# Dividing one expansion of queries by bank pairs around a turn of x, in a polysketch attention + GELU MLP kernel

## The chip, the cores and the metric

The kernel runs on one core of one Trainium2 chip. A core has several engines that run at the same time, each with its own queue of instructions: TensorE (PE in the profile, with its weight loads as PEld), VectorE (DVE), ScalarE (ACT), GpSimd (POOL), and SyncE (SP), which here only issues DMAs. TensorE writes its products to PSUM, a memory of eight banks per partition, and VectorE or ScalarE reads them from there. The metric is the device time of one execution, in microseconds (us); lower is better.

## The reference, cut to what matters

```python
# attention: q, k, v of (batch 4, heads 4, tokens 1088, 32), sketches S1, S2 of (8, 32)
def phi(x):
    a = einsum('rd,bhsd->bhsr', S1, x)
    b = einsum('rd,bhsd->bhsr', S2, x)
    return einsum('bhsi,bhsj->bhsij', a, b).reshape(..., 64)
q_p, k_p = phi(q), phi(k)
kv  = einsum('bhsf,bhsd->bhfd', k_p, v);  z = sum(k_p, axis=2)
num = einsum('bhsf,bhfd->bhsd', q_p, kv)
den = einsum('bhsf,bhf->bhs', q_p, z)[..., None] + 1e-06
x   = (num / den) -> (batch*tokens, heads*32) = (4352, 128)
# MLP: w_in (128, 2048), w_out (2048, 128)
h   = x @ w_in
out = (0.5 * h * (1 + erf(h / sqrt(2)))) @ w_out
```

Every token gets 64 features, the products of two sketches of length 8. Attention is linear: keys and values are first summed to a 64 x 32 table per head (`kv`) and a vector (`z`), and each query token then needs a product with both and a division. Its result `x` is the input of the MLP.

## The kernel before, in words

The 1024 main tokens of each of the four batches are cut into two chunks of 512 tokens, so there are eight main chunks, and a ninth takes the 64 remaining tokens of all batches. Chunks 0 and 1 belong to batch 0. The MLP takes each chunk in 16 steps (`fi`): a step multiplies `x` of the chunk by 128 columns of `w_in` (`hidden`, L715, the matmul is at L721), ScalarE applies the GELU (L728), and a projection by `w_out` follows (`project`, L845, the matmul is at L856, or `two_products`, L792, with a Strassen-like scheme for later chunks).

At the start there is no `x`, so the first 23 us or so prepare batch 0: keys, `kv`, queries of chunk 0, numerators of chunk 0, and at the same time the queries of chunk 1. All instructions of an engine keep the order in which the program writes them (the last lines of the kernel add such a dependency). So each engine's queue is what the text says, from top to bottom.

The passages around the change:

- `expand_products` (L533) makes the features of the queries of one chunk. A matmul there has a weight of 32 rows x 64 columns (`Srep`) and 256 moving columns (`qT`). There are 16 of them: `s` (0, 1) for the two factors of the feature product, `g` (0 to 3) for the four tokens that are in the four 32-row groups of `qT`, `c` (0, 1) for the two 64-row halves of the output. The row group that is read is `g`, and the half of the output is `c`. The output of group `g` goes to one PSUM bank of its own, `B_of[n, g // 2][:, g % 2]`, with both `s` side by side. `B_of[n, 0]` and `B_of[n, 1]` are each a pair of banks from a pool of two such pairs (`work_banks`, L67).
- `expand_copy` (L548) copies the first factor out of a bank pair with ScalarE (the line that shows in the profile is L550), and `expand_multiply` (L552, shown as L555) multiplies by the second factor with VectorE.
- `numerators_by_token` (L648, shown as L656) multiplies features by `kv` and `z`. For chunk 0 it writes tokens 0 and 1 to two banks named `h_ps` and tokens 2 and 3 to two named `o_ps`.
- `divide` (L663) divides the numerators with VectorE (L673, L674, L679) and so makes `x_tok` in two halves; the denominators of the second half are copied by ScalarE (`denominators`, L683, shown as L687).
- `turn_half_apart` (L690) turns such a half, which has tokens in partitions, into `xT` with channels in partitions: two transposes on TensorE (L694), each into its own bank, and two copies out of PSUM (L696), one by ScalarE and one by VectorE.
- `first_hidden` (L730, shown as L735) makes the first hidden step of a chunk in two parts of 256 columns, one for each half of `xT`.

The main text has these calls in this order (L938 to L959): numerators of chunk 0, denominators, the expansion of chunk 1, the divisions, the two turned halves, the two first hidden parts, the copies and products of the expansion. The loop over steps then begins (L962 on). Its first four turns make hidden steps 0 to 3 of chunk 0, and the fourth also makes the numerators, divisions and turns of chunk 1.

The weights `w_in` and `w_out` come as 64-bit numbers and are rounded on the chip, piece by piece (`Rounding`, L243), with VectorE and ScalarE; such instructions (L260 to L297) stand between the others in both queues.

Of the kernel before, what the change touches and what calls it, by code (L numbers as in the profile page):

```python
# [8 lines left out]
FP = mybir.dt.float32  # L9
# [7 lines left out]
def kernel(  # L17
# [30 lines left out]
    CW = JC * 128  # L48
    G = 128 // 32
# [11 lines left out]
    att = ctx.enter_context(tc.tile_pool(name="att", bufs=2))  # L61
# [5 lines left out]
    def work_banks():  # L67

        return wps.tile([128, 2, CW], FP, name="w_ps")

    def work_bank():
        return work_banks()[:, 0]
# [4 lines left out]
    def hidden_bank():  # L77
        return hps.tile([128, CW], FP, name="h_ps")

    def out_bank():  # L80
        return ops.tile([128, CW], FP, name="o_ps")


    by_act, by_dve, by_pool = act.copy, dve.tensor_copy, pool.tensor_copy
# [432 lines left out]
    qT, qp, xT = {}, {}, {}  # L517
# [12 lines left out]

    A, B_of = {}, {}

    def expand_products(n):  # L533


        W = width[n]
        for i in range(2):
            B_of[n, i] = work_banks()
        for s in range(2):
            for g in range(G):  # L540
                for c in range(NP):
                    rows = slice(g * D, (g + 1) * D)
                    pe.matmul(B_of[n, g // 2][c * F:(c + 1) * F, g % 2, s * W // 2:(s + 1) * W // 2],  # L543
                              lhsT=Srep[rows, s].rearrange("p i j -> p (i j)"),
                              rhs=qT[n][rows, 2 * c:2 * c + 2].rearrange("p r j t -> p r (j t)"), start=True, stop=True)
        qp[n] = att.tile([128, 2, CW], FP, name="q_pT")

    def expand_copy(n, i):  # L548
        A[i] = att.tile([128, 2, CW // 2], FP, name="A_sb")
# [113 lines left out]
    def divide(n, banks, tokens, by_head_pair, den=None):  # L663

        g = len(tokens) * 2
        given = den is not None
        if not given:
            den = att.tile([128, NP, JC * 2], FP, name="den_tok")[:, :, :g]
        parts = [slice(c, c + 1) for c in range(NP)] if by_head_pair else [slice(0, NP)]
        nd = [(banks[c.start][:, None] if by_head_pair else banks)[:, :, :g * C].rearrange("p b (g c) -> p b g c", c=C)  # L670
              for c in parts]
        for c, x in zip(parts, nd) if not given else ():
            dve.tensor_scalar(out=den[:, c], in0=x[:, :, :, D], scalar1=1e-6, scalar2=None, op0=AX.add)  # L673
        dve.reciprocal(out=den, in_=den)  # L674
        for i in range(len(tokens) // 2):
            to = x_half(n, tokens[0] // 2 + i).rearrange("p j (c r) d -> p c j r d", c=NP)
            for c, x in zip(parts, nd):
                for b in range(c.stop - c.start):
                    dve.tensor_mul(out=to[:, c.start + b], in0=x[:, b, i * 4:i * 4 + 4, 0:D].rearrange("p (j r) d -> p j r d", r=2),  # L679
                                   in1=den[:, c.start + b, i * 4:i * 4 + 4].rearrange("p (j r) -> p j r", r=2)[:, :, :, None]  # L680
                                   .broadcast_to([128, 2, 2, D]))
# [5 lines left out]
            act.activation(out=den[:, c], in_=ps[:, :JC * C].rearrange("p (g c) -> p g c", c=C)[:, :, D], func=ACT.Copy, bias=1e-6)  # L687
        return den

    def turn_half_apart(n, i, banks):  # L690
        if i == 0:
            xT[n] = att.tile([128, CW], FP, name="xT", bufs=3)
        for j, ps in enumerate(banks):
            pe.transpose(ps[:, :128], in_=x_tok[n, i][:, j].rearrange("p h d -> p (h d)"), identity=ident)  # L694
        for j, ps in enumerate(banks):
            (by_act, by_dve)[j](out=xT[n][:, i * 256 + j * 128:i * 256 + (j + 1) * 128], in_=ps[:, :128])  # L696

    def turn_half(n, i, ps, copy):
        if i == 0:
# [190 lines left out]
    bank = work_bank()  # L890
# [15 lines left out]
    banks = [out_bank(), out_bank()]  # L906
    key_features(0, 0, banks)
    key_features(0, 1, [hidden_bank(), hidden_bank()], by_pool=(1,))
    widen_v(1)
    widen_v_rem(0)  # L910
    expand_products(0)
    for i in range(2):
        query_features(0, i)
# [27 lines left out]
        numerators_by_token(0, banks, tokens)  # L941
    den = denominators(nd[1])
    w_in[1].exponents()
    expand_products(1)
    for banks, tokens, by in zip(nd, parts, (None, den)):
        divide(0, banks, tokens, by_head_pair=True, den=by)
    for half, bank in enumerate((hidden_bank, out_bank)):
        turn_half_apart(0, half, [bank(), bank()])
    w_in[1].mantissa_fields()
    for half in range(2):  # L950
        first_hidden(0, half)
# [210 lines left out]
    for t in range(len(steps) + LAG):  # L1162
        if t < 4:
# [9 lines left out]
            if t == 3:  # L1173
                banks = work_banks()
# [23 lines left out]
        if t < len(steps):  # L1198
            n, fi = steps[t]
            hidden(n, fi, by_halves=t >= 18 and (n < NMAIN or fi < 5))  # L1200
        if t < len(steps) and steps[t][0] < NMAIN and steps[t][1] % NB == NB - 1:
            n, b = steps[t][0], steps[t][1] // NB
# [50 lines left out]
```

## Time and profile before

| what | value |
|---|---|
| median of 3 runs | 259.6 us (259.22 to 259.74) |
| the profiled execution's own time | 258.95 us |
| its span, first to last instruction | 257.1 us |
| PE busy | 253.1 us (98%), 2331 instructions |
| DVE busy | 151.0 us (59%), 313 instructions |
| ACT busy | 115.2 us (45%), 224 instructions |
| POOL busy | 164.1 us (64%), 173 instructions |
| mean TensorE clock granted | 1.000 |

The profile is of one execution. Starts are counted from the first instruction. A matmul of 32-bit numbers shows as two matmul instructions with a weight load each, so the 16 matmuls of an expansion show as 32. The end of a matmul is modelled[...]; the distance from one start to the next says more about what TensorE can take than the recorded duration does.

### The profile page before, as it was taken

What the parts mean: (1) busy time and instruction counts of PE and PEld (TensorE: products, weight loads), DVE (VectorE), ACT (ScalarE), POOL (GpSimd) and SP (SyncE); (2) the same over time, 40 slices, a digit from 0 to 9 for tenths busy, and PEclk for the clock granted to TensorE, in tenths of its full rate; (3) what the DMA queues carried; (4) which work ended last, traced back from release to release, by engine and by line L of the source; (5) the groups of instructions that cost most, each with busy time, mean ns of one, the idle gap of its engine ahead of it and who ended that gap; (6) DMA issues with size and microseconds to landing.
All of it is one profiled execution on the core that took longest, in us unless ns stands there. A gap on an engine that the chain in (4) does not pass through costs nothing.

```text
span 257.1 us, 5763 instructions
## 1 busy us (share of the span) xinstructions
PE 253.1 (98%) x2331; PEld 135.2 (53%) x2331; DVE 151.0 (59%) x313; ACT 115.2 (45%) x224; POOL 164.1 (64%) x173
## 2 busy tenths in 40 slices
PE   8999999999999999999999999999999999999995
PEld 7856444255454545454444455445544444445794
DVE  3896888969698996580278976399307000700330
ACT  4675766533535333533335332623444334433442
POOL 3504007799968777587758774787758777877300
PEclk9999999999999999999999999999999999999999
DMA  7479738720000101101000002000200200020020
GB/s 209 138 213 378 163 93 223 208 75 13 3 0 15 28 1 26 18 13 30 3 0 3 0 13 35 0 1 3 41 3 8 32 3 1 7 36 0 3 41 20
DMA packets 29594, 13.48 MB, mean 52 GB/s; under 512 B 21888, under 2 KB 27776, under 8 KB 29568
## 3 DMA queue, kind: packets, MB, share of 16 engines
q1 hardware_dynamic: 29392, 13.05, 20.4%
q8 instruction: 18, 0.29, 0.5%
q10 hardware_dynamic: 176, 0.07, 0.1%
q14 instruction: 8, 0.07, 0.1%
HBM read 10.88 MB, written 2.23 MB: 51 GB/s over the span
## 4 chain that ended last, share of the span: by engine, by line
PE 98%; ACT 0%; issue 0%
PE h_ps L721 45%; PE o_ps L805 33%; PE o_ps L856 5%; PE w_ps L853 3%; PE w_ps L437 1%; PE w_ps L578 1%; PE w_ps L888 1%; PE w_ps L633 1%; PE w_ps L543 1%; PE o_ps L426 1%; PE h_ps L735 1%; PE w_ps L976 1%; PE w_ps L656 0%; PE h_ps L333 0%; PE w_ps L333 0%; PE w_ps L467 0%
## 5 line engine op out<-in xcount | busy, mean ns | idle before, releaser
L721 PE MATMUL h_ps<-xT,w_in 128*64 128x512 f32 (+3 forms) x514 | 136.9, 576 | 0.0
L728 ACT ACTIVATE block<-h_ps 128x512 f32<-128x512 f32 (+1 forms) x128 | 73.0, 571 | 117.3 <-PE h_ps L721 115.3
L721 PEld LDWEIGHTS h_ps<-xT,w_in 128*64 128x64 f32 (+1 forms) x514 | 41.9, 142 | 30.6 <-issue 11.8
L805 PE MATMUL o_ps<-block,w_out 128*64 128x256 f32 x224 | 57.5, 379 | 0.0
L770 POOL TENSOR_TENSOR bits_low<-block 128x512 f32<-128x512 f32 x28 | 35.9, 1283 | 27.8 <-ACT block L728 27.8
L805 PEld LDWEIGHTS o_ps<-block,w_out 128*64 128x64 f32 x224 | 30.5, 137 | 38.0 <-issue 27.5
L771 POOL TENSOR_TENSOR bits_a<-block 128x512 f32<-128x512 f32 x28 | 35.8, 1278 | 12.0 <-ACT block L728 11.9
L820 DVE COPY sums<-o_ps 64x256 f32<-64x256 f32 x8 | 3.3, 416 | 60.7 <-PE o_ps L805 60.7
L772 POOL TENSOR_TENSOR bits_e<-bits_a,block 128x512 f32<-128x512 f32 x28 | 36.0, 1286 | 2.2
L773 POOL TENSOR_TENSOR bits_m<-block,bits_e 128x512 f32<-128x512 f32 x28 | 35.8, 1278 | 2.2
L805 PE MATMUL o_ps<-bits_a,small 128*64 128x256 f32 x112 | 28.8, 379 | 0.0
L805 PE MATMUL o_ps<-bits_low,small 128*64 128x256 f32 x112 | 28.8, 379 | 0.0
L805 PE MATMUL o_ps<-block,small 128*64 128x256 f32 x112 | 28.8, 379 | 0.0
L805 PE MATMUL o_ps<-bits_m,w_out 128*64 128x256 f32 x112 | 28.7, 379 | 0.0
L805 PEld LDWEIGHTS o_ps<-block,small 128*64 128x64 f32 x112 | 15.2, 137 | 17.9 <-issue 10.8
L805 PE MATMUL o_ps<-bits_e,small 128*64 128x256 f32 x112 | 17.0, 383 | 0.0
L856 PE MATMUL o_ps<-g,w_out 128*128 128x512 f32 (+1 forms) x34 | 16.5, 572 | 0.0
L805 PEld LDWEIGHTS o_ps<-bits_m,w_out 128*64 128x64 f32 x112 | 15.3, 137 | 0.0
L805 PEld LDWEIGHTS o_ps<-bits_a,small 128*64 128x64 f32 x112 | 15.2, 137 | 0.0
L805 PEld LDWEIGHTS o_ps<-bits_low,small 128*64 128x64 f32 x112 | 15.2, 137 | 0.0
L590 DVE STREAM_TRANSPOSE w_ps<-w_ps 128x512 f32<-128x512 f32 (+1 forms) x7 | 4.8, 687 | 17.1 <-ACT xT L644 12.7
L805 PEld LDWEIGHTS o_ps<-bits_e,small 128*64 128x64 f32 x112 | 7.7, 137 | 10.6 <-issue 8.8
(195 smaller groups left out, 303.7 us busy)
## 6 DMA issues: line engine op xcount, KB each, us to landing
block<-in_moe_w_in_dram SPq DMA_DIRECT2D x3, 512.0 KB, 8.3
block<-in_moe_w_out_dram SPq DMA_DIRECT2D x3, 512.0 KB, 12.3
k<-in_k_dram SPq DMA_DIRECT2D x12, 128.0 KB, 3.0
v<-in_v_dram SPq DMA_DIRECT2D x12, 128.0 KB, 3.3
q<-in_q_dram SPq DMA_DIRECT2D x24, 64.0 KB, 1.9
out_dram<-oT SPq DMA_DIRECT2D x21, 64.0 KB, 2.2
k<-in_k_dram SPq DMA_DIRECT2D x2, 256.0 KB, 3.2
q<-in_q_dram SPq DMA_DIRECT2D x2, 256.0 KB, 3.7
```

What stands on the lines that cost most here:

```text
L426: pe.matmul(ps[c * F:(c + 1) * F, r * 2 * D:r * 2 * D + C], lhsT=flat(k_p[0, r][:, t, c * 4 + ch * 2 + one]), rhs=v_aug[r][:, c, i, :C], s ...
L590: dve.transpose(out=tok, in_=ps[:, :, :H2])
L721: pe.matmul(ps[rows, :W], lhsT=w[:, rows], rhs=xT[n][:, :W], start=True, stop=True)
L728: act.activation(out=g_of[n, fi][:, :W], in_=ps[:, :W], func=ACT.Gelu)
L770: pool.tensor_sub(out=s[3], in0=a11, in1=a21)
L771: pool.tensor_add(out=s[1], in0=a21, in1=a22)
L772: pool.tensor_sub(out=s[2], in0=s[1], in1=a11)
L773: pool.tensor_sub(out=s[4], in0=a12, in1=s[2])
L805: pe.matmul(acc[n][bank][half * 64:(half + 1) * 64, col:col + HW], lhsT=fixed, rhs=moving, start=opens and e == 0 and name in "4715", stop ...
L820: dve.tensor_copy(out=N[lo, 0, one], in_=a0[lo, one])
L853: pe.matmul(o_of[n][i][:, :128], lhsT=g[:, i * 128:(i + 1) * 128], rhs=w_tile(w_out_sb, fi), start=first, stop=final)
L856: pe.matmul(o_of[n][:, cols], lhsT=w_tile(w_out_sb, fi), rhs=g[:, cols], start=first, stop=final)
```

## The change

`expand_products` gets a second argument, the token groups `g` that it is to treat. The expansion of chunk 1 is called twice: with groups 0 and 1, which fill the bank pair `B_of[1, 0]`, and with groups 2 and 3, which fill `B_of[1, 1]`. The turn of the first half of chunk 0's `x` stands between the two calls, and the turn of the second half after the second. The two copies of the first half out of PSUM are both made by ScalarE, where VectorE made one of them; the copies of the second half are as before. The buffer `q_pT` of a chunk is taken ahead of the first group's matmuls, no longer after the matmuls. All other calls of `expand_products` treat all four groups at once.

```diff
-    def expand_products(n):
-
+    def expand_products(n, group=range(G)):
 
         W = width[n]
-        for i in range(2):
+        if group[0] == 0:
+            qp[n] = att.tile([128, 2, CW], FP, name="q_pT")
+        for i in (group[0] // 2, group[-1] // 2) if len(group) > 2 else (group[0] // 2,):
             B_of[n, i] = work_banks()
         for s in range(2):
-            for g in range(G):
+            for g in group:
                 for c in range(NP):
                     rows = slice(g * D, (g + 1) * D)
                     pe.matmul(B_of[n, g // 2][c * F:(c + 1) * F, g % 2, s * W // 2:(s + 1) * W // 2],
                               lhsT=Srep[rows, s].rearrange("p i j -> p (i j)"),
                               rhs=qT[n][rows, 2 * c:2 * c + 2].rearrange("p r j t -> p r (j t)"), start=True, stop=True)
-        qp[n] = att.tile([128, 2, CW], FP, name="q_pT")
...
-    def turn_half_apart(n, i, banks):
+    def turn_half_apart(n, i, banks, copies=(by_act, by_dve)):
         if i == 0:
             xT[n] = att.tile([128, CW], FP, name="xT", bufs=3)
         for j, ps in enumerate(banks):
             pe.transpose(ps[:, :128], in_=x_tok[n, i][:, j].rearrange("p h d -> p (h d)"), identity=ident)
         for j, ps in enumerate(banks):
-            (by_act, by_dve)[j](out=xT[n][:, i * 256 + j * 128:i * 256 + (j + 1) * 128], in_=ps[:, :128])
+            copies[j](out=xT[n][:, i * 256 + j * 128:i * 256 + (j + 1) * 128], in_=ps[:, :128])
...
     den = denominators(nd[1])
     w_in[1].exponents()
-    expand_products(1)
+    expand_products(1, range(0, 2))
     for banks, tokens, by in zip(nd, parts, (None, den)):
         divide(0, banks, tokens, by_head_pair=True, den=by)
-    for half, bank in enumerate((hidden_bank, out_bank)):
-        turn_half_apart(0, half, [bank(), bank()])
+    turn_half_apart(0, 0, [hidden_bank(), hidden_bank()], (by_act, by_act))
+    expand_products(1, range(2, G))
+    turn_half_apart(0, 1, [out_bank(), out_bank()])
     w_in[1].mantissa_fields()
```

## The prediction

> **What bounds the kernel now.** I read the page's chain first: it says what sets the end.
>
> ```profile
> PE 98%; ACT 0%; issue 0%
> ```
>
> TensorE is on the chain nearly throughout, so whatever moves its queue moves the end, unless a later wait of TensorE absorbs it. The starts of its matmuls after 23 us hardly leave a gap (each 512-column pass follows 0.43 us after the last), so nothing after 23 us can give time back. The question is what the change does to TensorE between 12 and 23 us. The timeline of that stretch (start, duration, engine, line, operation, idle before) has what matters:
>
> ```profile
> 12.65 0.49 DVE L679 TENSOR_TENSOR x_tok<-h_ps,den_tok 128x128 f32<-128x128 f32 x2
> 13.35 0.49 DVE L679 TENSOR_TENSOR x_tok<-o_ps,den_tok 128x128 f32<-128x128 f32 x2
> 13.55 0.44 PE L694 MATMUL h_ps<-ident,x_tok 128*128 128x128 f32 x2
> 13.99 0.41 PE L694 MATMUL o_ps<-ident,x_tok 128*128 128x128 f32 x2
> 14.32 0.27 ACT L696 COPY xT<-o_ps 128x128 f32<-128x128 f32 x1
> 14.44 0.29 DVE L696 COPY xT<-o_ps 128x128 f32<-128x128 f32 x1
> 14.46 1.10 PE L735 MATMUL h_ps<-xT,w_in 128*128 128x256 f32 x4
> 14.49 1.08 ACT L550 COPY A_sb<-w_ps 128x512 f32<-128x512 f32 x2
> 15.60 0.60 ACT L728 ACTIVATE g<-h_ps 128x512 f32<-128x512 f32 x1
> 16.29 0.19 PEld L721 LDWEIGHTS h_ps<-xT,w_in 128*128 128x128 f32 x1 [0.70 <-ACT g L728]
> ```
>
> Half 0 of x_tok is ready at 13.14, half 1 at 13.84. The first transpose starts at 13.55, well after half 0: it waits for the expansion ahead of it. The second turn starts at 13.99 because it waits for half 1. The second turn's copy by ScalarE (14.32) has two expansion copies behind it, and behind those the first GELU (15.60), which has to free a PSUM bank before hidden step 2 may start (the 0.70 us wait). So ScalarE's queue, set off by the second turn, decides here together with TensorE.
>
> How the expansion uses the array shows in the busy windows of its line alone (window, length, matmuls under way, weight loads):
>
> ```profile
> 12.40:12.62 0.22, 0.12 (x8) 0.13 (x16) 1.00 0.27 74
> 12.62:12.76 0.14, 0.14 (x8) 0.11 (x16) 1.00 0.00 0
> 12.76:12.97 0.21, 0.21 (x16) 0.18 (x8) 1.00 0.00 0
> 12.97:13.19 0.22, 0.22 (x16) 0.18 (x8) 1.00 0.00 0
> 13.19:13.54 0.35, 0.35 (x16) 0.00 (x0) 1.00 0.32 18
> ```
>
> Eight matmuls start within 0.05 us at 12.50; none follows until 12.76, when the next eight start (16 are then under way by the modelled ends), and so at 12.98 and 13.19. The 32 passes go in **four rounds of eight**, 0.27, 0.215 and 0.215 us apart. A pass of 256 columns alone takes the same 0.215 us: the passes of L735 start at 14.75, 14.97 and 15.18. So a round is one pass on each of eight parts of the array.
>
> **What the Trainium skill says.** "TensorEngine Tiling (Array Packing)", section Tiling Modes: the array split into 32-row, 64-column parts gives eight; each is tied to its own input and output partitions; and "Changing tiling mode (not just tile) drains the TensorE". The trace agrees on both: eight starts at once, and gaps where the shape changes (0.14 us from the last round's pass to the transposes: 13.19 + 0.215 = 13.41, start 13.55). "TensorE: Matmul & The Clock Gate", section The mechanism: matmuls start and end in program order, so the second turn can't overtake what is put ahead of it. The trace shows no start out of the text's order here. "PSUM — Partial Sum Buffer", section Engine vs sequencer instructions: ScalarE's and VectorE's queues are strictly first in, first out, as the timeline shows too; nothing passes a waiting copy.
>
> **The change, part by part.**
>
> *The expansion is divided.* Groups 0 and 1 lie in rows 0 to 63 of the array, groups 2 and 3 in rows 64 to 127. A call with two groups can use two row parts times two column parts: four of the eight. Its 8 matmuls are 16 passes, four at a time: again **four rounds**. Each half call lasts as long as the whole did, 0.27 + 3 x 0.215 = 0.91 us. The trace has no 32x64 pass by fours, so the bounds: from two rounds (0.27 + 0.215 = 0.48 us, if eight could run anyhow) to four. The nearest rows are the 64x64 numerators (L656): starts come by fours, as many as such parts fit in the array. I take four rounds, since the groups have no other rows.
>
> *First half call*: starts at 12.50 as now, last round at 13.19. The first turn follows at 13.55 and 13.71 as now; half 0 has been ready since 13.14, so no wait appears. Cost: 0.
>
> *Second half call*, now between the turns: the last transpose takes one 128-column pass, half of 0.215, so TensorE is free at 13.71 + 0.11 = 13.82. Change of shape: before, 128-row hidden step to 64-row numerators, 17.69 + 0.43 = 18.12, start 18.21: 0.10 us. Then 0.91, then 0.14 for the change back to transposes. Sum 1.15: the second turn starts at 13.82 + 1.15 = 14.97 instead of 13.99. The existing wait for half 1 (13.82 to 13.99) hides 0.17 of it; the rest, **0.98 us**, is new.
>
> *What is behind the second turn*: ScalarE's copy of half 1 moves from 14.32 to 15.30, its two expansion copies end at 16.55 instead of 15.57, the first GELU starts at 16.58. VectorE's copy (14.44) and everything behind it, the rounding of the second w_in piece and the two expansion products (16.09), move by 0.98 too. Hidden step 2 waits for the GELU: +0.98.
>
> *First hidden part*: it now waits 0.23 us for the copies of half 0 and 1 (14.12 + 0.11 = 14.23 to 14.46). After the change the copies of half 0 are done under the second half call (the second ScalarE copy ends about 14.45), so part 0 starts right behind the second turn, at 15.10 + 0.11 = 15.21. That 0.23 buys nothing: part 1 needs the copies of half 1, which end at 14.73 + 0.98 = 15.71 and let it start about 15.83. It ends about 16.53; the GELU is held to 16.58 by ScalarE's own queue besides.
>
> *Both copies of half 0 by ScalarE*: one copy of 0.27 us more on ScalarE, hidden by its idle time before 15.30; if that cover were gone (second turn at 13.99), it would end at about 14.45 and push the next copy from 14.32 by 0.13. VectorE loses 0.29 us of work, which it did in idle time. Cost: 0.
>
> *q_pT taken earlier; banks*: no instruction. The second pair's last reader was ScalarE's copy of turned queries (11.54, 0.59), done at 12.13. No DMA is moved; the queues of SP and POOL keep their order. Cost: 0.
>
> Sum: +0.98 us. From 16.3 to 23 us every TensorE wait is for ScalarE or VectorE work that moves as much, and after that TensorE has no gap, so all of it reaches the end. The profiled execution would go from 258.95 to 259.93 us (span 257.1 to 258.1). It lies 0.65 under the median of the runs shown; on the median: 259.6 + 0.98 = **260.6 us**.
>
> **The rivals.**
>
> *The likeliest* (72%): as above, 260.6; its own range is 260.3 to 260.9, from shape changes of 0.05 to 0.20 us each and the spread of the runs.
>
> *The halves are really halves* (12%; not slower): eight passes run at once whatever their rows, so each call has two rounds. The first call's last pass is over at 12.98; the first turn waits for half 0 (13.14) and starts about 13.27, is over at 13.54; 0.10 + 0.48 + 0.14 follow, and the second turn starts at 14.26: +0.27, so 259.9. With free changes of shape it would start at 14.02, next to today's 13.99: 259.6. It decides where a half call costs under 0.7 us. For it: the records overlap, 16 are under way at once. Against: the starts, which come in eights with a pause of one pass. A gain is bounded in any case: the second turn can't start before half 1 is ready, and ScalarE's chain to the GELU starts there. A gain past 0.2% needs 0.52 us from somewhere that the profile doesn't show (3%).
>
> *Partly absorbed* (6%): some wait between 16 and 23 us doesn't move along, such as the 0.70 us one ahead of hidden step 2, and gives back half: 260.1. Against: its releaser, the GELU, moves too.
>
> *Dearer* (7%): changes of shape drain longer with four parts idle, or the second call's first round waits for its weights: 0.2 us at each of two places, 261.0; or a rounding step slips behind in ScalarE's queue, up to 261.3.
>
> **How the numbers follow.** I take the likeliest case's time. The range of 259.9 to 261.1 leaves out the better part of the halves case and the tail of the dear one, under 2 in 10. A measurement of this kernel tells about 0.2% (0.52 us: 259.08 to 260.12) from no change. Slower: 70 of the likeliest's 72, 2 of the absorbed 6, 7 of the dear: 0.79. Same: 12 of the halves case, and 2 and 4 that remain: 0.18. Faster: 0.03.
>
> **What would show it.** In the profile after: the expansion's matmuls start by fours in twice four rounds, eight rounds in all, with the first turn at about 13.5 and the second at about 15.0; ScalarE's first GELU near 16.6; PE's busy time some 1 us up. The first hidden part starts without a wait, and the second part follows after a pause. Wrong, if starts come in eights or a half call lasts about 0.5 us; if the second turn starts near 14.3; or if hidden step 2 starts less late than the second turn.

## The result, and the profile after

| | before | after |
|---|---|---|
| median of 8 runs each | 259.39 us (258.84 to 259.74) | 260.18 us (259.79 to 260.58) |
| profiled execution's own time | 258.95 us | 260.55 us |
| its span | 257.1 us | 258.8 us |
| first matmul of chunk 1's expansion | 12.50 us | 13.17 us |

The ratio is 1.0033 with a 95% interval of 1.0021 to 1.0045: 0.5 to 1.2 us slower. A second set of runs, with five of the changed kernel (after_again below), gave 1.0046 (1.0034 to 1.0059).

The two profiled executions differ by 1.60 us, more than the change makes. The last row of the table shows why: chunk 1's expansion is the first TensorE work that differs, and the profile after reaches it 0.68 us later. That is a difference in the first 12 us, in which both kernels do the same; the runs of other variants below, whose times are those of the kernel before, also get there between 12.9 and 13.5 us. So I compare the traces **from the last start of the numerators' matmuls (L656), just ahead of the expansion**, to the end of the span: 244.80 us before and 245.75 after, **0.95 us** more. The first GELU comes 0.93 us later on that count, hidden step 2 0.95. Nothing is given back after that: every TensorE start from hidden step 2 to the end comes 0.95 to 0.96 us later than its counterpart before.

The timeline after (start, duration, engine, line, operation, idle before) has this where the prediction showed the turns of before:

```profile
13.17 1.09 PE L544 MATMUL w_ps<-qT,Srep 32*64 32x256 f32 x16
14.20 0.44 PE L694 MATMUL h_ps<-ident,x_tok 128*128 128x128 f32 x2
14.56 0.43 ACT L696 COPY xT<-h_ps 128x128 f32<-128x128 f32 x2 [0.64 <-PE h_ps L694]
14.56 1.09 PE L544 MATMUL w_ps<-qT,Srep 32*64 32x256 f32 x16
15.59 0.44 PE L694 MATMUL o_ps<-ident,x_tok 128*128 128x128 f32 x2
15.86 1.31 PE L735 MATMUL h_ps<-xT,w_in 128*128 128x256 f32 x4
15.95 0.27 ACT L696 COPY xT<-o_ps 128x128 f32<-128x128 f32 x1 [0.96 <-PE o_ps L694]
16.06 0.29 DVE L696 COPY xT<-o_ps 128x128 f32<-128x128 f32 x1 [1.54 <-PE o_ps L694]
16.11 1.08 ACT L550 COPY A_sb<-w_ps 128x512 f32<-128x512 f32 x2
16.47 0.30 PEld L735 LDWEIGHTS h_ps<-xT,w_in 128*128 128x128 f32 x2 [0.41 <-ACT xT L696]
17.21 0.60 ACT L728 ACTIVATE g<-h_ps 128x512 f32<-128x512 f32 x1
```

Each half of the expansion, with 16 passes, lasts 1.09 us, where all 32 passes together took 1.12 us before. The first hidden part starts right behind the second turn, but the second part then waits 0.41 us for the copies of half 1 (the view names ScalarE's, but that is over at 16.22 and VectorE's, which ends last, at 16.35). The busy windows of the expansion's line alone show how each half runs (window, its length, busy time of matmuls with the number under way, the same of weight loads; then the clock, the DMA share and GB/s, which are not used here):

```profile
13.08:13.30 0.22, 0.13 (x4) 0.13 (x8) 1.00 0.27 74
13.30:13.43 0.13, 0.13 (x4) 0.08 (x7) 1.00 0.00 0
13.43:13.64 0.21, 0.21 (x8) 0.15 (x4) 1.00 0.00 0
13.64:13.86 0.22, 0.22 (x8) 0.15 (x4) 1.00 0.00 0
13.86:14.18 0.32, 0.32 (x8) 0.00 (x0) 1.00 0.02 6
14.50:14.72 0.22, 0.16 (x4) 0.16 (x8) 1.00 0.38 98
14.72:14.82 0.10, 0.10 (x4) 0.05 (x4) 1.00 0.94 317
14.82:15.03 0.21, 0.21 (x8) 0.15 (x4) 1.00 0.96 341
15.03:15.25 0.22, 0.22 (x8) 0.15 (x4) 1.00 1.09 386
```

Four matmuls start, none follows until 0.27 us later, then again four (eight under way): four rounds of four, and the second half runs the same way. Four of the array's eight parts have no pass in any of the eight rounds.

### The profile page after: what moved, and what is told of

The parts are those of the page before. It is cut to its first block, busy times and chain, and to the rows that moved or that the text cites. A ratio compares the mean times of both kernels' runs of the same rounds, so it can differ in the third digit from the quotient of the medians.

```text
span 258.8 us, 5763 instructions
## 1 busy us (share of the span) xinstructions
PE 254.8 (98%) x2331; PEld 136.0 (53%) x2331; DVE 150.8 (58%) x312; ACT 115.5 (45%) x225; POOL 164.3 (63%) x173
## 4 chain that ended last, share of the span: by engine, by line
PE 98%; ACT 0%; issue 0%
PE h_ps L721 45%; PE o_ps L805 33%; PE o_ps L856 5%; PE w_ps L853 3%; PE w_ps L437 1%; PE w_ps L888 1%; PE w_ps L578 1%; PE w_ps L633 1%; PE w_ps L544 1%; PE o_ps L426 1%; PE h_ps L735 1%; PE w_ps L977 1%; PE w_ps L656 0%; PE h_ps L333 0%; PE w_ps L333 0%; PE w_ps L467 0%
```

## The experiments

All variants keep the computation; they differ in order and engines only. The table gives, from each variant's trace, starts and ends in us, counted from the last start of the numerators' matmuls, and the measured ratio to the kernel before. "4 of 8" stands for four rounds of eight passes, "turn" for the turn of the first half of `x`, where it stands between or ahead.

| kernel | rounds of the expansion | second turn | first GELU | end of span | ratio, 95% interval |
|---|---|---|---|---|---|
| before | 4 of 8 | 1.64 | 3.25 | 244.80 | |
| after | 4 of 4, turn, 4 of 4 | 2.56 | 4.18 | 245.75 | 1.0033 (1.0021 to 1.0045) |
| after_again | the same | 2.57 | 4.19 | 245.74 | 1.0046 (1.0034 to 1.0059) |
| split_only | 4 of 8 | 1.65 | 3.28 | 244.80 | 1.0004 (0.9996 to 1.0012) |
| by_factor | 2 of 8, turn, 2 of 8 | 1.90 | 3.52 | 245.08 | 1.0013 (1.0003 to 1.0022) |
| by_column | 4 of 4, turn, 4 of 4 | 2.56 | 4.18 | 245.75 | 1.0045 (1.0033 to 1.0057) |
| between | turn, 4 of 8 | 2.33 | 3.95 | 245.50 | 1.0023 (1.0013 to 1.0033) |
| copies_only | 4 of 8 | 1.65 | 3.28 | 244.79 | 0.9997 (0.9988 to 1.0007) |
| early_copy | 4 of 4, turn, 4 of 4 | 2.56 | 4.18 | 245.75 | 1.0026 (1.0015 to 1.0038) |
| groups_outer | 4 of 8 | 1.64 | 3.29 | 244.80 | 0.9998 (0.9988 to 1.0008) |
| columns_outer | 4 of 8 | 1.65 | 3.28 | 244.81 | 0.9999 (0.9991 to 1.0008) |

On this count the end agrees within 0.02 us among kernels that do the same there, and the first GELU within 0.05, so it tells more than the times do. Its differences to the kernel before, over 259.5 us, lie in every interval of the last column.

**The changed kernel again.**

> The changed kernel again, beside the three that follow. Theory (P): an expansion's passes run at once only on distinct parts of the array, so each bank-pair half takes four rounds of four. From the expansion's first matmul to the second turn's first transpose 2.41 us (1.49 in the kernel before), to the first GELU 4.03 us (3.10 before); time +0.8 to +1.0 us over the kernel before.

The expected distances are those of the first trace, so this tells only that they repeat. They do: 2.41 us from the expansion's first matmul to the second turn (the table counts 0.15 us more), end +0.94 us. The runs gave 0.9 to 1.5 us, an interval that holds the upper half of what was expected.

**The division without the turn in between** (against the changed kernel; the copies are again as in the kernel before).

```diff
     expand_products(1, range(0, 2))
+    expand_products(1, range(2, G))
...
-    turn_half_apart(0, 0, [hidden_bank(), hidden_bank()], (by_act, by_act))
-    expand_products(1, range(2, G))
-    turn_half_apart(0, 1, [out_bank(), out_bank()])
+    for half, bank in enumerate((hidden_bank, out_bank)):
+        turn_half_apart(0, half, [bank(), bank()])
```

> The expansion divided by bank pairs, both halves one behind the other, both turns after them, and the copies as in the kernel before. P: the ordering of the matmuls alone costs. Twice four rounds of four, of which some may merge where the halves meet, since rows 0 to 63 and 64 to 127 are distinct parts: 6 to 8 rounds. 2 to 4 rounds more of 0.215 us, less the 0.17 us that the second turn waited anyway: +0.26 us (6), +0.48 (7) or +0.69 (8). Rival (H), a call's time goes with the number of its matmuls: four rounds as before, 0.0 us; the cost of the change was then in the turn between.

P's cost of 0.26 us or more did not come; the rival's 0.00 us did. The rival's reason isn't the cause, though, as the windows of this kernel show (same columns as above):

```profile
13.30:13.35 0.05, 0.04 (x4) 0.04 (x4) 1.00 0.00 0
13.35:13.52 0.17, 0.17 (x8) 0.17 (x16) 1.00 0.35 96
13.58:13.76 0.18, 0.18 (x16) 0.18 (x8) 1.00 0.00 0
```

Four matmuls start at 13.31, four more at 13.36, and the next eight not before 13.58. The second four belong to the second half: in the trace, the weight load that carries the wait for the second bank pair is the fifth to start, at 13.36, though it belongs to the ninth matmul of the text. The two halves run side by side, in the same four rounds: the passes of the second half start 0.05 us behind those of the first, ahead of the first half's remaining passes, although the text has all of the first half before them. So the division by bank pairs costs nothing in itself, and neither does `q_pT` taken earlier, which this kernel keeps. The division costs when the turn stands between the halves: in the changed kernel no pass of the second half starts ahead of the transposes, though the four parts that it needs are free (the transposes start at 14.20 and 14.36, the second half at 14.56). No run separates whether it is the change of shape that holds the passes back, or that a transpose takes all the parts.

**Divided by factors, the turn between** (the cuts are against the kernel before). Both halves use all eight parts.

```diff
-    def expand_products(n):
+    def expand_products(n, factors=range(2), cols=range(NP)):
...
-        for s in range(2):
+        for s in factors:
             for g in range(G):
-                for c in range(NP):
+                for c in cols:
...
-    expand_products(1)
+    expand_products(1, range(0, 1))
...
-    for half, bank in enumerate((hidden_bank, out_bank)):
-        turn_half_apart(0, half, [bank(), bank()])
+    turn_half_apart(0, 0, [hidden_bank(), hidden_bank()], (by_act, by_act))
+    expand_products(1, range(1, 2))
+    turn_half_apart(0, 1, [out_bank(), out_bank()])
```

> The changed kernel, but its expansion divided by the two factors (s = 0, then s = 1) instead of by bank pairs: each half has all eight parts, two rounds. The turn stands between as in the change. P: the first half is over at 0.48 us; the first turn waits for half 0 of x_tok and starts 0.79 us after the expansion's start; then 0.10 + 0.48 + 0.11 us to the second turn, at about 1.75 us instead of 1.49: +0.26 us over the kernel before, 0.65 less than the change. If the turn between the halves is what costs (H), it stays at about +0.9 us.

The second turn came at 1.75 us on that count, 1.90 in the table: +0.26 as worked out, and +0.29 at the end. The timeline of TensorE in this kernel:

```profile
13.08 0.69 PE L543 MATMUL w_ps<-qT,Srep 32*64 32x256 f32 x16
13.87 0.41 PE L695 MATMUL h_ps<-ident,x_tok 128*128 128x128 f32 x2
14.21 0.69 PE L543 MATMUL w_ps<-qT,Srep 32*64 32x256 f32 x16
14.83 0.44 PE L695 MATMUL o_ps<-ident,x_tok 128*128 128x128 f32 x2
```

The same turn, and again 16 passes ahead of it and 16 behind it, each group 0.69 us long instead of 1.09: eight start at 13.08 and eight at 13.34, then eight at 14.21 and eight at 14.48. About two thirds of the change's 0.95 us are therefore the idle parts; the rest is the turn's place: two more changes of shape, and a second turn that has to come after work for which its old wait was too short. This version isn't faster than the kernel before either.

**Divided by output columns, the turn between.** As above with `cols=range(0, 1)` and `cols=range(1, 2)` in place of the factors.

> As by_factor, but divided by the column halves of the output (c = 0, then c = 1): each half has all four row groups, one column half, four of the eight parts. P: four rounds of four in each half, as in the change: second turn 2.41 us after the expansion's start, +0.9 us. Rival (R), that only the row groups limit, so that a call which reads all four runs in two rounds: second turn at about 1.75 us, +0.26 us.

2.41 us again, four rounds of four, and the same end as the change to 0.01 us:

```profile
13.28 1.09 PE L543 MATMUL w_ps<-qT,Srep 32*64 32x256 f32 x16
14.30 0.44 PE L695 MATMUL h_ps<-ident,x_tok 128*128 128x128 f32 x2
14.67 1.09 PE L543 MATMUL w_ps<-qT,Srep 32*64 32x256 f32 x16
15.69 0.44 PE L695 MATMUL o_ps<-ident,x_tok 128*128 128x128 f32 x2
```

It is the number of free parts that counts, not whether the halves differ in rows or in columns, and not the bank pairs.

**The expansion undivided, between the turns.**

```diff
-    expand_products(1)
...
-    for half, bank in enumerate((hidden_bank, out_bank)):
-        turn_half_apart(0, half, [bank(), bank()])
+    turn_half_apart(0, 0, [hidden_bank(), hidden_bank()], (by_act, by_act))
+    expand_products(1)
+    turn_half_apart(0, 1, [out_bank(), out_bank()])
```

> The expansion undivided, all 16 matmuls between the two turns; the copies of half 0 both by ScalarE as in the change. P: four rounds only. The first turn waits for half 0 of x_tok and starts 0.79 us after the point where the expansion started before (0.13 us or so behind the numerators in the kernel before), is over at 1.05; 0.10 + 0.91 + 0.11 us follow; second turn at 2.17 us on that count against 1.49: +0.68 us, 0.25 less than the change, though TensorE stands idle ahead of the first turn. H: no cheaper than the change.

The second turn came 0.69 us later than in the kernel before, the end 0.71. TensorE's timeline shows the wait ahead of the first turn that this order brings:

```profile
14.23 0.41 PE L694 MATMUL h_ps<-ident,x_tok 128*128 128x128 f32 x2 [0.72 <-DVE den_tok L674]
14.57 1.12 PE L543 MATMUL w_ps<-qT,Srep 32*64 32x256 f32 x32
15.62 0.44 PE L694 MATMUL o_ps<-ident,x_tok 128*128 128x128 f32 x2
```

The view names L674, but the transposes read half 0 of `x_tok`, whose last product (L679) ends at 14.08, 0.15 us ahead of the first of them. Even with TensorE idle for 0.72 us this kernel ends 0.25 us ahead of the change.

**The copies alone**, on the kernel before.

```diff
-    for half, bank in enumerate((hidden_bank, out_bank)):
-        turn_half_apart(0, half, [bank(), bank()])
+    turn_half_apart(0, 0, [hidden_bank(), hidden_bank()], (by_act, by_act))
+    turn_half_apart(0, 1, [out_bank(), out_bank()])
```

> The kernel before with both copies of half 0 by ScalarE and nothing else. P: ScalarE's second copy ends at about the time at which the second turn's copy could start; 0.0 to +0.13 us, likeliest +0.02. If the extra copy on ScalarE is a cause of the change's cost: +0.27 us.

Nothing: the end is the same to 0.01 us. The extra copy on ScalarE is no cause. The second turn's first copy starts 0.01 us later than in the kernel before.

**ScalarE's first expansion copy ahead of the second turn's copy**, on the changed kernel.

```diff
+    expand_copy(1, 0)
     expand_products(1, range(2, G))
...
-    expand_copy(1, 0)
     w_in[1].mantissas()
```

> The changed kernel with the first expansion copy on ScalarE moved ahead of the second turn's copy, into ScalarE's idle time. P: TensorE's first hidden part ends at the same time as ScalarE's queue came free, so the first GELU starts no earlier: 0 to -0.05 us against the change. If ScalarE's queue alone sets the first GELU: up to -0.55 us.

ScalarE's timeline in this kernel:

```profile
14.98 0.60 ACT L550 COPY A_sb<-w_ps 128x512 f32<-128x512 f32 x1
16.05 0.27 ACT L696 COPY xT<-o_ps 128x128 f32<-128x128 f32 x1 [0.47 <-PE o_ps L694]
16.21 0.59 ACT L550 COPY A_sb<-w_ps 128x512 f32<-128x512 f32 x1
17.31 0.60 ACT L728 ACTIVATE g<-h_ps 128x512 f32<-128x512 f32 x1 [0.50 <-PE h_ps L735]
```

The copy fits in idle time, and ScalarE now waits 0.50 us for the first hidden part, yet the GELU starts at the same distance (4.18) and the end is the same. ScalarE's queue and TensorE reach that point together; relieving ScalarE gives nothing.

**The order of the matmuls within one expansion.** split_only left open how a matmul gets ahead of earlier ones of the text. Two further orders of the kernel before, for chunk 1 only; the sort key is 1 (`g`) in groups_outer and 2 (`c`) in columns_outer:

```diff
-        for s in range(2):
-            for g in range(G):
-                for c in range(NP):
+        loops = [(s, g, c) for s in range(2) for g in range(G) for c in range(NP)]
+        if n == 1:
+            loops.sort(key=lambda x: x[1])
+        for s, g, c in loops:
```

> The kernel before, with the 16 matmuls of chunk 1's expansion in another order in the text: group g outermost, so that four matmuls in a row read the same 32 rows. The runs so far left open why the halves of split_only, one behind the other in the text, ran side by side in four rounds. If passes start in the order of the text (T), only two distinct parts stand side by side, and two at the joints: 13 to 16 rounds, some 2 us more. If each row group takes its own passes and doesn't wait for those of other rows (L): four rounds of eight, second turn 1.64 us after the last numerator as in the kernel before, 0.0 us.

> The same with the column half c outermost: eight matmuls for one half of the output, then eight for the other, every row group in both. T: 6 to 8 rounds, second turn 0.26 to 0.69 us later than in the kernel before. If the parts of one row group wait for each other in the order of the text while row groups are independent (L), the same 6 to 8 rounds; if each of the eight parts is independent (L8), four rounds and 0.0 us.

Both have four rounds of eight and the end of the kernel before. The windows of groups_outer:

```profile
13.25:13.40 0.15, 0.14 (x8) 0.14 (x16) 1.00 0.39 109
13.40:13.51 0.11, 0.11 (x8) 0.11 (x14) 1.00 0.00 0
13.52:13.73 0.21, 0.21 (x16) 0.21 (x10) 1.00 0.00 0
```

Eight are under way by 13.40, though the text has eight passes for the first group's two parts before any of the second group. In the trace, the groups start in pairs at 13.257, 13.283, 13.310 and 13.337, so 0.027 us apart, and each goes on from there at its own 0.27, 0.215 and 0.215 us. T is out by both runs and L by columns_outer; L8 holds: each of the eight parts takes its own passes and waits only for its own.

The first starts tell a little more. In the kernel before, where the text names the eight parts one after the other, they start one step of 0.0067 us apart. Elsewhere a part's first start lies as many such steps behind the expansion's first as there are matmuls ahead of it in the text: 4 steps (0.027 us) for each further group in groups_outer, 8 steps (0.053 us) for the second half in split_only and for the second column half in columns_outer. Had the passes been sorted into rounds beforehand, one step between all eight, as in the kernel before, would be expected. The starts fit matmuls that arrive in the text's order and then wait only for their own part; what holds them there, the trace doesn't show.

## Why the prediction was right, and where not

*Four rounds in each half call*: right. 13.17, 13.44, 13.66 and 13.87, then 14.56, 14.83, 15.05 and 15.26; by_column shows the same with other halves of the array, by_factor the two rounds that eight free parts give. The reason that I gave, that the groups have no other rows, is only half of it: split_only shows that the missing parts would be filled by the other half's passes if the turn did not stand between. The cost is of division and turn together, not of the division.

*First half call and first turn at no cost*: right. The first turn starts 1.02 us after the expansion's first matmul, 1.05 before.

*The second half call's sum*, the term that was mis-sized: 1.15 us expected from the end of the first turn to the second; measured 0.10 for the first change of shape (14.36 + 0.11 = 14.47 to 14.56), 0.91 for the rounds, 0.11 for the change back (15.26 + 0.215 = 15.48 to 15.59): 1.12. The last term was 0.03 too large, because the prediction counted it from the first start of a round. Counted from the last start of the last round, a change to transposes takes 0.09 us before and after; but a round of eight takes 0.047 us to get started, a round of four 0.020. The first turn comes 0.03 earlier for the same reason, so the second turn is 0.92 us late, not 0.98.

*The existing wait hides 0.17 us, the wait of the first hidden part buys nothing*: right. Part 0 starts 0.11 us behind the second transpose and part 1 waits for the copies, 3.33 us after the expansion's start. That this is just what was worked out (15.83 - 12.50) is luck: the second turn came 0.06 earlier, its two transposes lay 0.03 further apart than before (0.165 against 0.138), and from the last copy's end to part 1 it took 0.15, not the 0.12 assumed.

*ScalarE's queue sets the GELU*: the time is near (+0.93 against +0.98), the emphasis not quite right: early_copy shows that TensorE alone would hold the GELU there too. The prediction had the two 0.05 us apart.

*Both copies by ScalarE at no cost*: right, by copies_only. Its side estimate of 0.13 us without idle time to cover the copy was too large: 0.01 was measured, since two such copies in a row take 0.43 us (14.56 in the timeline after), not twice 0.27.

*All of it reaches the end*: right, +0.95 in the trace against 0.98. TensorE's busy time from the numerators on grew by the same 0.98 us (241.55 to 242.53). The forecast of 260.6 us was made on a median of 259.6; the larger set of runs has 259.39 before and 260.18 after, a difference of 0.79 whose interval, 0.5 to 1.2, holds 0.95. The median alone would not have decided: 260.18 lies just below the likeliest case's own range (260.3 to 260.9) and closest to the partly absorbed case (260.1), because the base was 0.2 us too high and the difference came out 0.2 us below the sum. The traces decide.

*The halves are really halves* (12%): out, by the starts. What it would have cost was worked out well, though: by_factor, whose halves have two rounds, came to +0.26 against the +0.27 of this case. *Partly absorbed*: out, hidden step 2 and the end are 0.95 us late, no less than the second turn (0.92). *Dearer*: out; the changes of shape took 0.10 and 0.11 us as the prediction counts them.

*What the prediction took from the Trainium skill*: that a change of shape drains the array ("TensorEngine Tiling (Array Packing)", section Tiling Modes) agrees with the pauses of 0.10 and 0.11 us here. That matmuls start in program order ("TensorE: Matmul & The Clock Gate", section The mechanism) isn't borne out within one shape: split_only, groups_outer and columns_outer show starts out of the text's order. It holds where the prediction used it, for the turns between the halves.

## What to carry to other kernels

Packed small matmuls kept the whole array at work when there was work for every part between two changes of the array's shape; their order within that stretch didn't matter here. To put other work in the middle, divide so that each piece still covers all parts (here by factor, 0.29 us, instead of by bank pair, 0.95 us; both figures include two more changes of shape). And first look whether the wait to be filled ends with data that come no sooner: the second turn's did, and none of the orders tried here beat the one before.

## What was not expected of the hardware

The parts of the array took up their work independently of the order in the text: in groups_outer all four row groups were at work within 0.09 us of the first matmul, in front of passes that the text has earlier. By the order of the text, which was one of the two rules on record for that run, it would have been 13 to 16 rounds and about 2 us more; four rounds and 0.00 us were measured.
